# Attention and two feed-forward layers on one core: masks in fewer operations, the first biases on VectorE, input words on another queue, a range test moved

## The chip, the cores and the metric

The kernel runs on one core of one Trainium2 chip. The metric is the device time of one execution in microseconds; lower is better. The compute engines are TensorE (PE in the profile, with its weight loads as PEld), VectorE (DVE), ScalarE (ACT) and GpSimd (POOL). SyncE (SP) only issues transfers; a name with a q, as SPq, is an engine's sequencer.

## The reference

The inputs are `q`, `k`, `v` of 2 batches, 8 heads, 768 positions and 64 dimensions, two integers `n_global` (8) and `n_local` (96), and two pairs of float64 weight matrices. A query sees a key if the key is among the first `n_global` or at most `n_local - 1` positions back:

```python
scores = scale * np.matmul(q, k.transpose(0, 1, 3, 2))
rel = pos[:, None] - pos[None, :]
is_global = pos[None, :] < int(n_global)
is_local = (rel >= 0) & (rel < int(n_local))
keep = is_global | is_local
dist = np.where(is_global & ~is_local, float(n_local), np.abs(rel))
scores = np.where(keep, scores - slopes[:, None, None] * dist, -1000000000.0)
a = softmax(scores); attn_out = np.matmul(a, v)
```

The result, as 1536 tokens of 512 channels, goes through two layers: `h = x @ w_in`, a gate (`h * sigmoid(h)` in the first, `h * clip(h + 3, 0, 6) / 6` in the second), `@ w_out`.

## The kernel before

The two integers are read on the chip, so the masks are made there. The kernel serves small values of both; at the end a flag tells whether the integers lie beyond that range, and a general version (`every_key`) runs if they do. Here they don't.

**The start.** The first block of code sets three warm-up matmuls going on TensorE (`warm_up(3)`), issues the transfers of the integers' words (`nwords`) and of the first units' inputs on SP's queue (`loads`, `loads_v`), and makes the masks on VectorE. `positions()` writes relative positions by GpSimd and converts them on VectorE. `patterns()` waits for the words, makes `ng` and `nl` of them, and writes two tiles of penalised distances: `distB` for the 128 keys of a block's own, and `distA` for 256 columns, which hold the 96 keys before, 32 global keys and the block's own. A key that is not kept gets at least the distance `FAR`. `biases(p)` multiplies both tiles with the slopes of the two heads of pair `p`, four operations on GpSimd, which gives `nbB` and `nbA`.

**Attention.** A unit is a batch, half of its positions and a pair of heads: 16 units, each in three steps of one query block. For every unit the keys and queries are transposed by TensorE (`stage_a`, into `psA`) and copied by ScalarE to `kt` and `qt`, with a small copy of the global keys by VectorE (L332). TensorE computes the scores (L359), VectorE adds the bias and takes the extreme (L370, into `z` and `mn`), ScalarE exponentiates (L374), GpSimd divides by the sums (L384), TensorE transposes the weights (`turn`, into `psT`), VectorE and ScalarE copy them to `pt`, and TensorE multiplies them with the values (`values`, `psO`). Steps are counted by `n`; `attention_loop(n)` runs them three to a unit, and `biases(u + 1)` comes with the first step of units 0 to 2.

**Feed-forward.** From step 17 on, matmul pieces of the first layer (`psH`, `psY`) are mixed in, and the float64 weights are fetched raw on SP's queue and decoded to two float32 parts by ScalarE, VectorE and GpSimd (`decode`, L103 to L148 and L983 to L1000).

**Order.** During attention TensorE, ScalarE and GpSimd follow the written order; the first block and, until attention ends, VectorE are ordered by a planner with costs of its own, which also orders SP's queue throughout. So an operation that is written late can come early: the range test `beyond()` is written at step 30, but its six operations run between those of `patterns()`. After attention VectorE follows the written order too. At step 77 all five sequencers read the flag that `beyond()` writes (L786):

```python
if n == PRE + 60:
    general = nc.values_load(flag[0:1, 0:1], min_val=0, max_val=2)
```

The functions that the diff touches, and their callers, with the profile's line numbers:

Of the kernel before, what the change touches and what calls it, by code (L numbers as in the profile page):

```python
# [10 lines left out]
F32 = mybir.dt.float32  # L11
F32R = mybir.dt.float32r
I32 = mybir.dt.int32
U32 = mybir.dt.uint32
AF = mybir.ActivationFunctionType
ALU = mybir.AluOpType
PSUM = bass.MemoryType.PSUM

P = 128
# [9 lines left out]
def attention_ffn_kernel(ctx, tc, q, k, v, n_global, n_local, w_in1, w_out1, w_in2, w_out2, out):  # L29
    nc = tc.nc  # L30
# [15 lines left out]
    keep = ctx.enter_context(tc.tile_pool(name="keep", bufs=1))  # L46
    ident = keep.tile([P, P], F32, name="ident", tag="ident")
    nval = keep.tile([P, 2], F32, name="nval", tag="nval")
    flag = keep.tile([P, 1], I32, name="flag", tag="flag")
    three = keep.tile([P, 1], F32, name="three", tag="three")  # L50

    main = ExitStack()
    first_half, second_half = ExitStack(), ExitStack()
    cpool = first_half.enter_context(tc.tile_pool(name="const", bufs=1, side="right"))
# [143 lines left out]
    PRE = 3 * NP + LAG + 1  # L198
# [50 lines left out]
    slopes = [2.0 ** (-8.0 * (h + 1) / H) for h in range(H)]  # L249
    FAR = 1e9 / slopes[-1]  # L250

    small = cpool.tile([P, 5], F32, name="small", tag="small")
    t1 = apool.tile([P, HB, 2, W], F32, name="pat1", tag="z", bufs=ZB)[:, 0]
    t2 = apool.tile([P, HB, 2, W], F32, name="pat2", tag="z", bufs=ZB)[:, 0]
    rel, tmp, glob, col = distA, t2[:, 0, :], t2[:, 1, :P], t2[:, 1, P:]

    def positions():

        reli, coli = t1[:, 0, :].bitcast(I32), t1[:, 1, :P].bitcast(I32)
        nc.gpsimd.iota(reli[:, :P], pattern=[[-1, P]], base=G0, channel_multiplier=1)  # L260
        nc.gpsimd.iota(reli[:, P:], pattern=[[-1, P]], base=0, channel_multiplier=1)
        nc.gpsimd.iota(coli, pattern=[[1, P]], base=0, channel_multiplier=0)
        nc.vector.tensor_copy(rel, reli)
        nc.vector.tensor_copy(col, coli)
        nc.vector.tensor_scalar(out=tmp, in0=rel, scalar1=0.0, scalar2=None, op0=ALU.is_ge)

    def patterns():

        low, up, high = nwords[:, :, 0], nwords[:, :, 1], small[:, 0:2]
        nc.vector.scalar_tensor_tensor(out=high, in0=low, scalar=0.0, in1=up, op0=ALU.is_lt, op1=ALU.add)  # L270
        nc.vector.scalar_tensor_tensor(out=nval, in0=high, scalar=4294967296.0, in1=low, op0=ALU.mult, op1=ALU.add)
        ng, nl = nval[:, 0:1], nval[:, 1:2]
        nc.vector.tensor_scalar(out=glob, in0=col, scalar1=ng, scalar2=None, op0=ALU.is_lt)
        nc.vector.scalar_tensor_tensor(out=tmp, in0=rel, scalar=nl, in1=tmp, op0=ALU.is_lt, op1=ALU.mult)

        def mask(dist, kept):
            nc.vector.tensor_scalar(out=kept, in0=kept, scalar1=-FAR, scalar2=FAR, op0=ALU.mult, op1=ALU.add)
            nc.vector.tensor_tensor(out=dist, in0=dist, in1=kept, op=ALU.max)


        nc.vector.scalar_tensor_tensor(out=distB, in0=rel[:, P:], scalar=nl, in1=tmp[:, P:], op0=ALU.subtract, op1=ALU.mult)
        nc.vector.tensor_scalar(out=distB, in0=distB, scalar1=nl, scalar2=None, op0=ALU.add)
        nc.vector.tensor_tensor(out=col, in0=tmp[:, P:], in1=glob, op=ALU.max)
        mask(distB, col)

        nc.vector.tensor_copy(tmp[:, G0:P], glob[:, :G])
        nc.vector.tensor_scalar(out=rel[:, G0:P], in0=rel[:, G0:P], scalar1=0.0, scalar2=nl, op0=ALU.mult, op1=ALU.add)
        mask(rel, tmp)

    def beyond():  # L290

        fl, ng, nl = small[:, 2:5], nval[:, 0:1], nval[:, 1:2]
        nc.vector.tensor_scalar(out=fl[:, 0:1], in0=nl, scalar1=1.0, scalar2=None, op0=ALU.is_lt)
        nc.vector.tensor_scalar(out=fl[:, 1:2], in0=nl, scalar1=float(NLOC_MAX), scalar2=None, op0=ALU.is_gt)
        nc.vector.tensor_scalar(out=fl[:, 2:3], in0=ng, scalar1=float(NGLOB_MAX), scalar2=None, op0=ALU.is_gt)
        nc.vector.tensor_tensor(out=fl[:, 0:1], in0=fl[:, 0:1], in1=fl[:, 1:2], op=ALU.add)
        nc.vector.tensor_tensor(out=fl[:, 0:1], in0=fl[:, 0:1], in1=fl[:, 2:3], op=ALU.add)
        nc.vector.tensor_copy(flag, fl[:, 0:1])
# [3 lines left out]
    def biases(p):  # L302

        nbs[p] = [cpool.tile([P, 2, w], F32, name=f"{n}{p}", tag=f"{n}{p}") for n, w in (("nbB", P), ("nbA", W))]
        for nb, dist in zip(nbs[p], (distB, distA)):
            for h in range(2):
                nc.gpsimd.tensor_scalar(out=nb[:, h, :], in0=dist, scalar1=slopes[2 * p + h], scalar2=1.0, op0=ALU.mult, op1=ALU.mult)


    KW = HB * SP  # L310
# [2 lines left out]
    def stage_a(u, part):  # L313

        b, half, p = units[u]
        rk, rq, rv, vp = raw[u]
        if part == 0:
            tr[u] = tuple(apool.tile([P, w], F32, name=f"{n}{u}", tag=n) for n, w in (("kt", KW), ("qt", TB)))
        kt, qt = tr[u]
        ps = bank("tr", f"psA{u}_{part}")  # L320
        src = rq if part else rk
        for i in range(HB):
            nc.tensor.transpose(ps[:, i * P:(i + 1) * P], src[:, i].rearrange("p h d -> p (h d)"), ident)
        if part:
            nc.scalar.mul(qt, ps[:, :TB], -1.0 / (D ** 0.5))
            return
        kt3 = kt.rearrange("p (t c) -> p t c", t=HB)
        nc.scalar.copy(kt3[:, :, :P], ps[:, :TB].rearrange("p (t c) -> p t c", t=HB))
        if half:
            nc.vector.tensor_copy(kt3[:, :HB - 1, P:], kept[b, p][:, G0:].unsqueeze(1).to_broadcast([P, HB - 1, G]))  # L330
        else:
            nc.vector.tensor_copy(kt3[:, :, P:], ps[:, :G].unsqueeze(1).to_broadcast([P, HB, G]))  # L332
            kept[b, p] = cpool.tile([P, P], F32, name=f"kept{u}", tag=f"kept{p}")
            nc.gpsimd.tensor_scalar(out=kept[b, p], in0=kt[:, KW - P:], scalar1=1.0, scalar2=1.0, op0=ALU.mult, op1=ALU.mult)
# [94 lines left out]
    def attention_loop(n):  # L429
        u, t = divmod(n, HB)  # L430
        for f in queue.pop(n, []):
            f()
        if u < len(units):
            if t == 0:
                scores(u)
                if u + 1 < NP:
                    biases(u + 1)
            exponentials(u, t)
            if t:
                normalise(u, *((0, 2), (2, 3))[t - 1])  # L440
        if t == 0 and 0 <= u - 2 < len(units):
            at(n + 1, values(u - 2))
            if u < len(units):
                loads_v(u)
        if n == 30:
            beyond()
        for f in rests.pop(n, []):
            f()
        if n == 2:
            warm_up(2)  # L450
        if t < 2 and u + 1 < len(units):
            stage_a(u + 1, t)
            if t and u + 3 < len(units):
                loads(u + 3)
# [277 lines left out]
    with tc.manual_schedule(engines=None):  # L732
        nc.vector.memset(three, 3.0)
        warm = fpool.tile([P, 512], F32, name="warm", tag="a")
        nc.vector.memset(warm, 0.0)
        warm_up(3)
        for i, ap in enumerate((n_global, n_local)):
            nc.sync.dma_start(nwords[:, i, :], ap.bitcast(I32).partition_broadcast(P))
        loads(0)
        make_identity(nc, ident)  # L740
        positions()
        loads(1)
        load_weights()
        loads_v(0)
        load_weights()
        loads(2)
        loads_v(1)
        load_weights()
        patterns()
        biases(0)  # L750
        stage_a(0, 0)
        stage_a(0, 1)
    todo = {when(i): f for i, f in enumerate(stream)}

    def loop(n):
        now[0] = n
        attention_loop(n)
        f = todo.get(n)
        if f:
            f[0](*f[1:])  # L760
        turns(n)
        for f in late.pop(n, []) + slots.pop(n, []):
            f()
# [8 lines left out]
    with tc.manual_schedule(engines={E.PE, E.Activation, E.Pool, E.DVE}):  # L772

        first_half.close()
        late_pool = second_half.enter_context(tc.tile_pool(name="late", bufs=1, side="right", reuse_waits="tile"))
        for b in range(2):
            whole_block(b)
        for n in range(end, when(len(stream) - 1) + 2):
            if n == when(first_piece[0, 3]):
                ready[0] = 2  # L780
            for l, c, early in ((0, 2, 0), (1, 1, 6)):
                if n == when(first_piece[l, c]) - early:
                    block_sums(l, n, n + early + 12)
            loop(n)
            if n == PRE + 60:
                general = nc.values_load(flag[0:1, 0:1], min_val=0, max_val=2)  # L786
    second_half.close()
# [245 lines left out]
```

## Time and profile before

| | us |
|---|---|
| median of 3 runs | 622.43 (622.29 to 622.67) |
| the profiled execution | 621.98 |
| its span, first to last instruction | 619.9 |
| TensorE busy | 599.9 (97% of the span) |
| VectorE, ScalarE, GpSimd busy | 471.5, 414.6, 161.4 |

A time line row gives the start, the duration, the engine, the line, the operation, what is written and read, how many instructions are merged, and in brackets the engine's idle time before it with what ended it. The durations of neighbours on one engine can overlap. A wait for several semaphores is put down to the one that came last by the profile.

### The profile page before, as it was taken

How to read it: one execution, taken by the hardware profiler on the slowest of the kernel's cores; microseconds unless marked ns; L12 is line 12 of the kernel's file. 1: busy time of each engine (PE TensorE's matmuls, PEld its weight loads, DVE VectorE, ACT ScalarE, POOL GpSimd, SP SyncE). 2: the span in 40 equal slices, each digit the busy share in tenths (PEclk: the TensorE clock that was granted, in tenths of full speed). 3: DMA queues.
4: the chain of work that ended last, by engine and by line, in shares of the span. 5: the costliest groups of instructions: out<-in, count | busy, mean ns of one | idle time of the engine just before them, and what ended most of it. 6: DMA issues, size and time to landing. Idle time of an engine off the chain costs nothing.

```text
span 619.9 us, 9396 instructions
## 1 busy us (share of the span) xinstructions
PE 599.9 (97%) x3144; PEld 492.1 (79%) x3144; DVE 471.5 (76%) x1036; ACT 414.6 (67%) x863; POOL 161.4 (26%) x241
## 2 busy tenths in 40 slices
PE   7789999999999999999999999999999999999996
PEld 3577788898887888888888878887788888888884
DVE  6988888636697767677766789987979797969453
ACT  4888888655576757575757776666667675757660
POOL 3987676821111111111111200011021112121200
PEclk9999999999999999999999999999999999999999
DMA  7876654584776777777777872476587777776544
GB/s 182 189 163 143 147 139 107 191 152 107 155 169 136 170 169 170 168 172 163 177 160 146 173 167 68 159 177 174 135 176 165 173 166 171 169 170 136 103 119 158
DMA packets 78679, 96.64 MB, mean 156 GB/s; under 512 B 52512, under 2 KB 52512, under 8 KB 78368
## 3 DMA queue, kind: packets, MB, share of 16 engines
q0 software_dynamic: 12576, 45.09, 38.9%
q1 hardware_dynamic: 66048, 50.87, 28.1%
q8 instruction: 27, 0.44, 0.3%
q14 instruction: 28, 0.23, 0.1%
HBM read 45.62 MB, written 3.15 MB: 79 GB/s over the span
## 4 chain that ended last, share of the span: by engine, by line
PE 36%; issue 26%; POOL 5%; DVE 2%; DMA 2%; ACT 1%; POOLq 0%; ACTq 0%; SPq 0%; DVEq 0%
PE psY L653 20%; PE psH L480 9%; POOL y L682 5%; PE psP_b L561 3%; PE psP_c L561 2%; PE psP_a L561 2%; DMA y<-st 1%; DMA raw<-in_moe_w_in_dram 1%; ACT st L678 0%; DVE g L511 0%; DVE da L995 0%; DVE wol L148 0%; DVE u L578 0%; DVE dc L134 0%; ACT da L103 0%
## 5 line engine op out<-in xcount | busy, mean ns | idle before, releaser
L682 POOL DMA_DIRECT2D y<-st x78 | 66.9, 858 | 364.9 <-ACT st L678 359.7
L678 ACT COPY st<-psY 128x512 f32<-128x512 f32 x156 | 91.5, 587 | 51.9 <-PE psY L653 47.9
L480 PE MATMUL psH<-xh,wih 128*128 128x512 f32 (+1 forms) x216 | 83.0, 384 | 1.2 <-DVE g L511 0.7
L480 PE MATMUL psH<-xh,wil 128*128 128x512 f32 (+1 forms) x216 | 82.5, 382 | 0.4 <-POOL wil L148 0.4
L480 PE MATMUL psH<-xl,wih 128*128 128x512 f32 (+1 forms) x216 | 82.6, 382 | 0.2 <-DVE xl L416 0.2
L653 PE MATMUL psY<-gh,woh 128*128 128x512 f32 (+1 forms) x160 | 61.4, 384 | 0.6 <-DVE mn L370 0.6
L653 PE MATMUL psY<-gh,wol 128*128 128x512 f32 (+1 forms) x160 | 60.6, 379 | 0.0
L653 PE MATMUL psY<-gl,woh 128*128 128x512 f32 (+1 forms) x160 | 60.5, 378 | 0.0
L653 PE MATMUL psY<-woh,gh 128*128 128x512 f32 x144 | 56.1, 390 | 0.5 <-ACT gh L517 0.5
L653 PE MATMUL psY<-woh,gl 128*128 128x512 f32 x144 | 56.1, 390 | 0.2 <-DVE gl L524 0.2
L653 PE MATMUL psY<-wol,gh 128*128 128x512 f32 x144 | 56.0, 389 | 0.0
L374 ACT ACTIVATE z<-z,mn 128x256 f32<-128x256 f32 (+1 forms) x96 | 46.3, 487 | 9.8 <-DVE mn L370 9.3
L384 POOL TENSOR_SCALAR z<-z,sm 128x256 f32<-128x256 f32 (+1 forms) x96 | 43.7, 475 | 21.4 <-DVE sm L380 16.0
L480 PEld LDWEIGHTS psH<-xh,wih 128*128 128x128 f32 x216 | 40.5, 188 | 9.5 <-ACT y L667 1.2
L103 ACT ACTIVATE da<-raw 128x512 f32<-128x512 f32 x64 | 43.0, 672 | 6.4 <-DMA raw<-in_moe_w_in_dram 5.9
L480 PEld LDWEIGHTS psH<-xl,wih 128*128 128x128 f32 x216 | 40.6, 188 | 7.9 <-DVE xl L416 0.5
L480 PEld LDWEIGHTS psH<-xh,wil 128*128 128x128 f32 x216 | 40.5, 188 | 8.0 <-POOL wil L148 0.8
L995 DVE SCALAR_TENSOR_TENSOR da<-raw,da 128x512 int32<-128x512 int32 x64 | 45.9, 717 | 1.0
L983 DVE TENSOR_SCALAR da<-da 128x512 f32<-128x512 f32 x64 | 29.8, 466 | 16.3 <-ACT da L103 16.2
L578 DVE TENSOR_TENSOR u<-psP_c,u 128x512 f32<-128x512 f32 x22 | 15.1, 688 | 34.5 <-ACT u L572 34.5
L502 ACT ACTIVATE a<-psH 128x512 f32<-128x512 f32 (+1 forms) x24 | 14.2, 590 | 40.3 <-PE psH L480 40.3
L521 DVE SCALAR_TENSOR_TENSOR gl<-a,gh 128x512 fp32r<-128x512 f32 (+1 forms) x34 | 23.2, 682 | 22.3 <-ACT gh L515 22.0
(186 smaller groups left out, 1497.8 us busy)
## 6 DMA issues: line engine op xcount, KB each, us to landing
y<-st POOLq DMA_DIRECT2D x78, 512.0 KB, 4.9
raw<-in_moe_w_in_dram SPq DMA_DIRECT2D x32, 512.0 KB, 4.2
raw<-in_moe_w_out_dram SPq DMA_DIRECT2D x32, 512.0 KB, 3.5
rk<-in_k_dram SPq DMA_DIRECT2D x32, 96.0 KB, 3.3
rq<-in_q_dram SPq DMA_DIRECT2D x32, 96.0 KB, 3.1
rv<-in_v_dram SPq DMA_DIRECT2D x32, 96.0 KB, 2.4
out_dram<-y SPq DMA_DIRECT2D x12, 256.0 KB, 2.3
xf<-xh SPq DMA_DIRECT2D x2, 1024.0 KB, 5.3
```

The costliest lines, as they stand in the source:

```text
L103: nc.scalar.activation(out=t["a"], in_=raws[n][:, :, 1].bitcast(F32), func=AF.Abs)
L374: nc.scalar.activation(out=z[:, t, h, :w], in_=z[:, t, h, :w], func=AF.Exp, bias=mn[:, t, h:h + 1], scale=-1.0, accum_out=sm[:, t, h:h + 1])
L384: nc.gpsimd.tensor_scalar(out=z[:, t, h, :w], in0=z[:, t, h, :w], scalar1=smt[u][:, t, h:h + 1], scalar2=1.0, op0=ALU.mult, op1=ALU.mult)
L480: nc.tensor.matmul(ps, a[:, kt, js], x[:, kt, n0:n1], start=n == 0, stop=n == 3 * KT - 1)
L521: nc.vector.scalar_tensor_tensor(out=gl[:, j, :], in0=t["a"], scalar=2.0, in1=gh[:, j, :].bitcast(F32), op0=ALU.mult, op1=ALU.subtract)
L561: nc.tensor.matmul(ps, a[:, 2 * k + q, f * P:(f + 1) * P], x, start=p in (1, 5) and n == 0, stop=n == 5, skip_group_check=True)
L578: nc.vector.tensor_tensor(out=u, in0=st["c"], in1=u, op=ALU.add)
L653: nc.tensor.matmul(ps[:, :rhs.shape[1]], lhs, rhs, start=n == 0, stop=n == 3 * FC - 1)
L678: nc.scalar.copy(st[:, m % 2, :], part)
L682: late.setdefault(n, []).append(lambda: nc.gpsimd.dma_start(y, st, accum_op=ALU.add))
L983: nc.vector.tensor_scalar(out=a, in0=a, scalar1=as_float(897 << 20), scalar2=as_float((1151 << 20) - 1), op0=ALU.max, op1=ALU.min)
L995: nc.vector.scalar_tensor_tensor(out=ai, in0=w1, scalar=-0x40000000, in1=ai, op0=ALU.bitwise_and, op1=ALU.bitwise_or)
```

## The change

Masks: the tests are negated (1 where a key is not kept), so that a fused operation can multiply them with `FAR` and add the distance at once; the helper `mask` goes, and three operations on the 128-column tile and two on the 256-column tile change. The maximum with `FAR` becomes a sum. Biases: those of pair 0 are made by VectorE, the others by GpSimd as before. Words: their two transfers are issued by ScalarE. The first `stage_a(0, 0)` is written ahead of `biases(0)`. The range test gets a tile of its own and is written at step 73 of the stage behind the attention, where VectorE follows the written order.

```diff
-    rel, tmp, glob, col = distA, t2[:, 0, :], t2[:, 1, :P], t2[:, 1, P:]
+    rel, tmp, glob, col, near = distA, t2[:, 0, :], t2[:, 1, :P], t2[:, 1, P:], t1[:, 1, P:]
-        nc.vector.tensor_scalar(out=tmp, in0=rel, scalar1=0.0, scalar2=None, op0=ALU.is_ge)
+        nc.vector.tensor_scalar(out=tmp, in0=rel, scalar1=0.0, scalar2=None, op0=ALU.is_lt)
...
-        nc.vector.tensor_scalar(out=glob, in0=col, scalar1=ng, scalar2=None, op0=ALU.is_lt)
-        nc.vector.scalar_tensor_tensor(out=tmp, in0=rel, scalar=nl, in1=tmp, op0=ALU.is_lt, op1=ALU.mult)
-
-        def mask(dist, kept):
-            nc.vector.tensor_scalar(out=kept, in0=kept, scalar1=-FAR, scalar2=FAR, op0=ALU.mult, op1=ALU.add)
-            nc.vector.tensor_tensor(out=dist, in0=dist, in1=kept, op=ALU.max)
-
-        nc.vector.scalar_tensor_tensor(out=distB, in0=rel[:, P:], scalar=nl, in1=tmp[:, P:], op0=ALU.subtract, op1=ALU.mult)
-        nc.vector.tensor_scalar(out=distB, in0=distB, scalar1=nl, scalar2=None, op0=ALU.add)
-        nc.vector.tensor_tensor(out=col, in0=tmp[:, P:], in1=glob, op=ALU.max)
-        mask(distB, col)
-
-        nc.vector.tensor_copy(tmp[:, G0:P], glob[:, :G])
-        nc.vector.tensor_scalar(out=rel[:, G0:P], in0=rel[:, G0:P], scalar1=0.0, scalar2=nl, op0=ALU.mult, op1=ALU.add)
-        mask(rel, tmp)
+        own, V = slice(P, W), nc.vector
+        V.scalar_tensor_tensor(out=tmp, in0=rel, scalar=nl, in1=tmp, op0=ALU.is_ge, op1=ALU.max)
+        V.tensor_scalar(out=glob, in0=col, scalar1=ng, scalar2=None, op0=ALU.is_ge)
+        V.scalar_tensor_tensor(out=near, in0=rel[:, own], scalar=nl, in1=tmp[:, own], op0=ALU.subtract, op1=ALU.mult)
+        V.tensor_tensor(out=near, in0=rel[:, own], in1=near, op=ALU.subtract)
+        V.tensor_tensor(out=col, in0=glob, in1=tmp[:, own], op=ALU.mult)
+        V.scalar_tensor_tensor(out=distB, in0=col, scalar=FAR, in1=near, op0=ALU.mult, op1=ALU.add)
+
+        V.tensor_copy(tmp[:, G0:P], glob[:, :G])
+        V.tensor_scalar(out=rel[:, G0:P], in0=rel[:, G0:P], scalar1=0.0, scalar2=nl, op0=ALU.mult, op1=ALU.add)
+        V.scalar_tensor_tensor(out=distA, in0=tmp, scalar=FAR, in1=rel, op0=ALU.mult, op1=ALU.add)
 
     def beyond():
 
-        fl, ng, nl = small[:, 2:5], nval[:, 0:1], nval[:, 1:2]
+        fl, ng, nl = beyonds, nval[:, 0:1], nval[:, 1:2]
...
-                nc.gpsimd.tensor_scalar(out=nb[:, h, :], in0=dist, scalar1=slopes[2 * p + h], scalar2=1.0, op0=ALU.mult, op1=ALU.mult)
+                (nc.gpsimd if p else nc.vector).tensor_scalar(out=nb[:, h, :], in0=dist, scalar1=slopes[2 * p + h], scalar2=1.0,
+                                                              op0=ALU.mult, op1=ALU.mult)
...
-        if n == 30:
-            beyond()
...
-            nc.sync.dma_start(nwords[:, i, :], ap.bitcast(I32).partition_broadcast(P))
+            nc.scalar.dma_start(nwords[:, i, :], ap.bitcast(I32).partition_broadcast(P))
...
         patterns()
+        stage_a(0, 0)
         biases(0)
-        stage_a(0, 0)
         stage_a(0, 1)
...
+            if n == PRE + 56:
+                beyond()
             if n == PRE + 60:
                 general = nc.values_load(flag[0:1, 0:1], min_val=0, max_val=2)
```

## Rows read from the trace of the kernel before

**Rows 1.** Stretches: length, then busy us of PE, PEld, DVE, ACT, POOL.
```profile
14.14:30.20 16.06, 12.45 (x115) 8.95 (x112) 14.73 (x62) 14.21 (x49) 15.60 (x31) 1.00 0.81 188
...
120.00:350.00 230.00, 229.43 (x1044) 191.54 (x1045) 157.46 (x282) 145.76 (x267) 38.55 (x43) 1.00 0.72 159
```

**Rows 2.** Time line of TensorE, 0 to 16 us.
```profile
1.51 5.59 PE L421 MATMUL psW<-warm 128*128 128x512 f32 x6 [1.51 <-DVE warm L735]
6.94 0.49 PE L323 MATMUL psA<-ident,rk 128*128 128x128 f32 x3
...
8.39 0.93 PE L359 MATMUL psS_S<-kt,qt 64*128 64x128 f32 x8 [0.63 <-ACT qt L325]
...
13.18 0.93 PE L359 MATMUL psS_S<-kt,qt 64*128 64x128 f32 x8 [0.58 <-ACT qt L325]
...
15.50 0.52 PE L323 MATMUL psA<-ident,rq 128*128 128x128 f32 x3 [0.42 <-DMA rq<-in_q_dram]
```

**Rows 3.** Time line of ScalarE, 0 to 16 us.
```profile
0.76 1.28 ACT L328 ACT_TABLE_LOAD   x1 [0.76 <-PEq L1015]
...
7.84 0.50 ACT L325 ACTIVATE qt<-psA 128x384 f32<-128x384 f32 x1
```

**Rows 4.** Time line of VectorE, 0 to 16 us.
```profile
4.78 0.16 DVE L270 SCALAR_TENSOR_TENSOR small<-nwords 128x2 f32<-128x2 int32 x1 [2.41 <-DMA nwords<-in_n_local_dram]
...
5.38 0.48 DVE L274 SCALAR_TENSOR_TENSOR pat<-distA,nval,pat 128x256 f32<-128x256 f32 x1
5.78 0.15 DVE L293 TENSOR_SCALAR small<-nval 128x1 f32<-128x1 f32 x1
...
5.90 0.35 DVE L281 SCALAR_TENSOR_TENSOR distB<-distA,nval,pat 128x128 f32<-128x128 f32 x1
...
6.49 0.29 DVE L283 TENSOR_TENSOR pat<-pat 128x128 f32<-128x128 f32 x1
...
6.81 0.23 DVE L277 TENSOR_SCALAR pat<-pat 128x128 f32<-128x128 f32 x1
...
7.51 0.40 DVE L277 TENSOR_SCALAR pat<-pat 128x256 f32<-128x256 f32 x1
...
8.29 0.25 DVE L332 COPY kt<-psA 128x96 f32<-128x96 f32 x1
9.46 0.29 DVE L370 CUSTOM_DVE_ANT_0 z<-psS_S,nbB 128x128 f32<-128x128 f32 x1 [0.92 <-POOL nbA L307]
...
14.14 0.29 DVE L370 CUSTOM_DVE_ANT_0 z<-psS_S,nbB 128x128 f32<-128x128 f32 x1 [0.17 <-PE psS_S L359]
```

**Rows 5.** Line 307 (biases), 0 to 30 us: count, ns min/median/max, first and last start.
```profile
L307 POOL TENSOR_SCALAR nbB<-distB x8: 294/299/499, 7.5 to 23.0; 128x128 f32<-128x128 f32 x8
L307 POOL TENSOR_SCALAR nbA<-distA x8: 406/408/907, 9.0 to 23.8; 128x256 f32<-128x256 f32 x8
```

**Rows 6.** Time line of SP's queue, 0 to 16 us.
```profile
0.76 0.39 SPq L738 DMA_DIRECT2D nwords<-in_n_global_dram  x1
...
1.67 0.96 SPq L228 DMA_DIRECT2D rk<-in_k_dram  x2
```

**Rows 7.** What TensorE waited for, 0 to 120 us: us in total, times, longest.
```profile
PE psT L394 <- DVE pt L399: 1.8, 3, 1.0
...
PE psO L412 <- DVE pt L399: 1.0, 1, 1.0
PE psA L323 <- DMA rq<-in_q_dram: 0.8, 2, 0.4
```

**Rows 8.** Line 786, the reads of the flag: count, ns, first and last start.
```profile
L786 SPq TENSOR_LOAD <-flag x1: 480/480/480, 45.6 to 45.6; - x1
...
L786 PEldq TENSOR_LOAD <-flag x1: 807/807/807, 161.0 to 161.0; - x1
```

**Rows 9.** Time line of VectorE, 155 to 163 us.
```profile
160.94 0.69 DVE L148 TENSOR_TENSOR wol<-dc,woh 128x512 fp32r<-128x512 f32 x1 [2.31 <-ACT woh L145]
```

**Rows 10.** Line 983 (a decode step), 0 to 40 us: count, ns min/median/max.
```profile
L983 DVE TENSOR_SCALAR da<-da x3: 427/868/967, 11.8 to 35.7; 128x512 f32<-128x512 f32 x3
```

More of the change, by code (lines that the diff above doesn't have):

```diff
@@ L49, in attention_ffn_kernel @@
     flag = keep.tile([P, 1], I32, name="flag", tag="flag")
+    beyonds = keep.tile([P, 3], F32, name="beyonds", tag="beyonds")
     three = keep.tile([P, 1], F32, name="three", tag="three")
@@ L250, in attention_ffn_kernel @@
     FAR = 1e9 / slopes[-1]
-    small = cpool.tile([P, 5], F32, name="small", tag="small")
+    small = cpool.tile([P, 2], F32, name="small", tag="small")
     t1 = apool.tile([P, HB, 2, W], F32, name="pat1", tag="z", bufs=ZB)[:, 0]
     t2 = apool.tile([P, HB, 2, W], F32, name="pat2", tag="z", bufs=ZB)[:, 0]
-    rel, tmp, glob, col = distA, t2[:, 0, :], t2[:, 1, :P], t2[:, 1, P:]
+    rel, tmp, glob, col, near = distA, t2[:, 0, :], t2[:, 1, :P], t2[:, 1, P:], t1[:, 1, P:]
     def positions():
```

## The prediction

> **What bounds the kernel now.** I read the stretches of the span first [rows 1]. From 120 to 350 us TensorE is busy 229.43 of 230.00 us: there only a change of TensorE's own work can pay. From 14.14 to 30.20 us it is busy 12.45 of 16.06, and GpSimd 15.60. All edits but one lie before 10 us. So the question is whether time saved there reaches TensorE, and whether it survives the stretch in which GpSimd is full.
>
> Then the time lines of the start. TensorE begins with the warm-up matmuls, from 1.51 us for 5.59, that is until 7.10; the first transposes follow at 6.94 without a wait shown [rows 2]. ScalarE's second copy of their results runs from 7.84 for 0.50 us [rows 3], and behind it, at 8.39, the first scores start [rows 2]. Their first eight matmuls take 0.93 us, until 9.32. VectorE's first addition of the bias starts at 9.46 [rows 4]. The trace puts its wait of 0.92 us down to GpSimd's bias tile, but it can only start behind the scores too. For the next unit the same step starts at 14.14, waiting for scores that began at 13.18 [rows 2, 4]: 13.18 plus 0.93 is 14.11, so it is 0.03 us behind them, against 0.14 here. GpSimd's biases hold up the first unit by at most 0.14 less 0.03, **0.11 us**.
>
> VectorE's mask work stands beside this chain, not in it: it waits 2.41 us for the input words, starts at 4.78 and is done when the key copy, at 8.29, has taken its 0.25: 8.54 [rows 4].
>
> **The change, part by part.**
>
> *Masks.* Before, VectorE ran 20 instructions from 4.78 to 8.54. Their durations sum to 4.93 us in 3.76 us, so neighbours overlap and a duration costs 0.76 of itself (a row of each kind stands in [rows 4], the first and the last of the 20 among them; six, of 0.15 to 0.16, are the range test). Afterwards, at those durations: two word operations 0.32, two fused operations on 256 columns 0.96, two on 128 columns 0.70, two with two tensors on 128 columns 0.58, one test on 128 columns 0.23, two short ones at no more than that 0.46, the key copy 0.25. Together 3.50 us.
>
> *First biases by VectorE.* The trace has no such step on this engine. The nearest are its operations with two constants, 0.23 us on 128 columns and 0.40 on 256 [rows 4]; two of each are 1.26. With the masks 4.76, times 0.76, 3.62: VectorE is done at 8.40. If nothing overlapped it would be 4.78 plus 4.76, 9.54. The scores end at 9.32 all the same, so I take nothing lost, and half of the 0.11 gained: **-0.05**. The upper bound: the key copy, which half of the eight score matmuls need, is planned last and ends at 9.54; half of 0.93 and the 0.03 follow, and the first bias step starts at 10.04 instead of 9.46, **+0.6**.
>
> *GpSimd relieved.* Four instructions go, two of about 0.30 and two of 0.41 us [rows 5], 1.4 us. They lie before 9.75, and GpSimd's full stretch begins only at 14.14, with the first unit's normalisation; that moves as the first unit does, so they count 0.
>
> *Input words on ScalarE's queue.* SP issues the words from 0.76 us and the first key load at 1.67 [rows 6], so all its early loads may come 0.9 us sooner. For unit 0 that is worth nothing: its transposes wait for the warm-up. Up to 120 us TensorE waits 0.8 us in all for query loads [rows 7], 0.42 of it at 15.50 [rows 2]. I count **-0.15** of that: GpSimd's and ScalarE's work of unit 0 and 1 is still under way behind it, so most of it would turn into another wait. The ends are 0 and -0.8. ScalarE is idle until its copies apart from a table load of 1.28 us [rows 3]; if the words were issued behind it, they would land 1.28 later, VectorE would be done at 9.68 instead of 8.40, and the first step would be 0.2 late, or 0.7 with the key copy last.
>
> The Trainium skill, DMA: Bandwidth & Descriptors, "Issuing engines are not separate DMA queues", says that issuing from several engines saves only issue time, since all transfers end on the same 16 DMA engines. By it, too, those 0.9 us are all that is to be had, and the words now meet the first key loads there; no row shows how much later they then land.
>
> *Range test.* Six instructions leave the gaps of the masks and go to step 73 of the loop, near 158 us, where VectorE sits idle for 2.31 us before 160.94 [rows 9]. Six of 0.16, not overlapped, are 1.0 us: hidden, and without that gap 1.0 us of VectorE where TensorE hardly waits for it. The flag is read by TensorE's sequencer at 161.0 us and by SP at 45.6 [rows 8]. SP must now wait for it until about 160; the weight loads behind it wait, by the code, for VectorE to have read an older piece, which it does after the test as well. I take 0; a test that came late by more than TensorE's queue holds would add what it is late.
>
> **Sum.** -0.05 and -0.15 are **-0.2 us** on the profiled execution's 621.98 us (a span of 619.9, with 2.1 around it). The median shown, 622.43, is 0.45 above that execution, so the forecast is 622.2. Measurements of this kernel tell about 0.2%, 1.24 us, from no change: I forecast no change, 621.7 to 622.6 with the small terms at their ends.
>
> **Rivals.** *(a) The shared port.* VectorE's new biases run beside GpSimd's biases of unit 1. One and the same VectorE operation takes 427 ns in one place and 967 in another [rows 10], and GpSimd's bias step 406 to 907 [rows 5], while both are busy. If each of four biases grew by 0.54, VectorE would be done at 8.40 plus 2.16, 10.56, and the first step would start 1.1 us late: 623.3. If they only waited for GpSimd's four steps, 1.4 us, it would be 9.80, 0.35 late, 622.6. Against it: GpSimd may be through with its own first. The Trainium skill, SBUF — State Buffer, "SBUF: two separate sides", has VectorE and GpSimd hold a shared pair of ports exclusively for a whole instruction, the loser waiting; by that rule the lower of the two prices holds, since the loser waits once for each step of the other.
>
> *(b) VectorE's order turns out better, and the time faster.* Up to about 120 us a planner orders VectorE and SP by its own clock, and a new head moves that clock. TensorE waits there 1.8 and 1.0 us for VectorE's copies of transposed weights [rows 7]; a decode step of 0.97 us planned ahead of such a copy makes such a wait [rows 10]. If half of the 2.8 went, with the loads' gain: -1.6, 620.8.
>
> *(c) The same order turns out worse, and the time slower.* One more decode step ahead of a copy costs up to 1.0 us [rows 7]; from two on it decides: +2.0 less 0.2, 624.2. VectorE is busy 14.73 of 16.06 us there [rows 1], so its order matters, for (b) and (c); against both, no work changes after 9.46 us.
>
> **Chances.** Forecast 0.58; (a) 0.12, within 0.2% as well; (b) 0.20; (c) 0.10. So faster 0.20, same 0.70, slower 0.10. The range is 620.8, the middle of (b), to 623.3, the top of (a), with the bound of +0.6 inside: it leaves out half of (b) and all of (c), 0.2.
>
> **What would show it.** After the change the warm-up should still end near 7.1 us and the first scores start near 8.4, the first bias step 0.9 to 1.1 us behind that, with VectorE done before; the first key load issued near 0.8; GpSimd's full stretch begin near 14.0; the range test sit in VectorE's gap before 161 us with no wait of TensorE. The prediction is wrong if TensorE's waits for VectorE from 14 to 120 us change by more than a microsecond, if the key copy comes behind the biases, or if masks start later than about 5.7 us, where the cover of 0.95 us (9.35 less 8.40) is used up.

## The result, and the profile after

| | before | after |
|---|---|---|
| median of 6 runs, lowest to highest (us) | 622.50, 621.90 to 623.88 | 626.57, 625.92 to 626.97 |
| ratio, 95% interval | | 1.0054, 1.0042 to 1.0065 |
| span of the profiled execution (us) | 619.9 | 623.8 |
| TensorE busy (us) | 599.9 | 605.4 |

The change makes the kernel 0.5% slower, about 4 us, where no change was forecast; 626.57 lies above the range and above the time of every rival. Below, ratios are compared and not times: the kernel before was timed again beside each group of experiments, and its medians lie from 622.5 to 623.4 us.

The stretches after, as in [rows 1]: TensorE is as full as before from 120 to 350 us, at the same granted clock, and GpSimd nearly as full from 14 to 30.

```profile
14.14:30.20 16.06, 12.71 (x116) 9.05 (x114) 13.89 (x64) 14.25 (x50) 15.19 (x31) 1.00 0.77 182
120.00:350.00 230.00, 229.68 (x1039) 190.32 (x1038) 156.49 (x286) 144.12 (x265) 38.43 (x43) 1.00 0.70 158
```

One number differs: in the same 230 us TensorE does 1039 matmuls instead of 1044. It is busy, and slower.

TensorE's time line of the start, beside [rows 2], and VectorE's, beside [rows 4]:

```profile
1.50 6.17 PE L419 MATMUL psW<-warm 128*128 128x512 f32 x6 [1.50 <-DVE warm L731]
...
8.96 0.93 PE L357 MATMUL psS_S<-kt,qt 64*128 64x128 f32 x8 [0.63 <-ACT qt L323]
...
15.31 0.49 PE L321 MATMUL psA<-ident,rq 128*128 128x128 f32 x3
...
17.04 1.06 PE L392 MATMUL psT<-ident,z 128*128 128x128 f32 x8 [1.02 <-DVE kt L330]
```
```profile
4.93 0.16 DVE L271 SCALAR_TENSOR_TENSOR small<-nwords 128x2 f32<-128x2 int32 x1 [2.56 <-DMA nwords<-in_n_local_dram]
...
8.55 0.26 DVE L330 COPY kt<-psA 128x96 f32<-128x96 f32 x1 [0.73 <-ACT kt L326]
8.72 0.43 DVE L304 TENSOR_SCALAR nbB<-distB 128x128 f32<-128x128 f32 x2
9.07 0.59 DVE L304 TENSOR_SCALAR nbA<-distA 128x256 f32<-128x256 f32 x2
9.92 0.29 DVE L368 CUSTOM_DVE_ANT_0 z<-psS_S,nbB 128x128 f32<-128x128 f32 x1 [0.26 <-PE psS_S L357]
```

The warm-up ends at 7.67 instead of 7.10, and all behind it is 0.57 later. The first bias step is 0.96 behind the first scores (1.07 before).

SP's queue, what TensorE waits for up to 120 us, and the range test (VectorE's time line, then the reads of the flag), beside [rows 6 to 9]:

```profile
0.76 0.98 SPq L229 DMA_DIRECT2D rk<-in_k_dram  x2
```
```profile
PE psT L392 <- DVE pt L397: 1.5, 3, 0.6
...
PE psT L392 <- DVE kt L330: 1.0, 1, 1.0
```
```profile
158.43 0.15 DVE L295 CAST flag<-beyonds 128x1 int32<-128x1 f32 x1
158.50 0.68 DVE L993 SCALAR_TENSOR_TENSOR da<-raw,da 128x512 int32<-128x512 int32 x1
160.93 0.69 DVE L149 TENSOR_TENSOR wol<-dc,woh 128x512 fp32r<-128x512 f32 x1 [1.74 <-ACT woh L146]
```
```profile
L784 SPq TENSOR_LOAD <-flag x1: 476/476/476, 158.6 to 158.6; - x1
...
L784 PEldq TENSOR_LOAD <-flag x1: 760/760/760, 161.0 to 161.0; - x1
```

None of this costs 4 us: TensorE's waits from 14 to 120 us sum to 7.3 us (8.5 before), those of them for VectorE to 4.8 (5.5). To find the place I took the start of the n-th matmul after, less that of the n-th before, all along the span: +0.55 us at 17 us, +0.06 at 46, about +0.1 up to 115, -0.01 from 155 to 196. Up to there the change has caught up with its late start. From 224 us on the difference grows, to about +1.6 at 347 us, stands still from 370 to 420, and reaches +4.11 at the end. Where it grows, TensorE works through the Strassen products: a layer's first matmul in seven block products in place of eight, some of them of sums and differences of blocks. `psP_a`, `psP_b` and `psP_c` collect them; `t2`, `t3`, `t4` are sums of the tokens (`xh`, `xl`), `ws` of the weights (`wih`, `wil`). Between them lies the layer's second matmul (`psY`, of the gated `g` and the weights `woh`, `wol`). The chain that ended last shows them in sixes; columns are start, length, what. First before, then after, the same work:

```profile
448.22 2.72 PE psY L653 x12
450.94 1.36 PE psP_b L561 x6
452.30 1.36 PE psY L653 x6
453.66 1.36 PE psP_c L561 x6
...
459.10 1.36 PE psP_a L561 x6
```
```profile
449.98 2.80 PE psY L649 x12
452.78 1.39 PE psP_b L557 x6
454.16 1.40 PE psY L649 x6
455.56 1.40 PE psP_c L557 x6
...
461.14 1.36 PE psP_a L557 x6
```

Six matmuls take 1.36 us in every piece before, 227 ns from the start of one to the start of the next; this is called their spacing below. After, they take 1.39 to 1.40 in some pieces, a spacing of 232 to 233, and 1.36 in others. One matmul overlaps the next, so its own duration is longer than the spacing. The durations of one product (count, ns min/median/max, first and last start), before and after:

```profile
L561 PE MATMUL psP_c<-xh,ws x80: 389/389/389, 228.5 to 590.6; 128*128 128x512 f32 x80
```
```profile
L557 PE MATMUL psP_c<-xh,ws x80: 389/396/400, 228.6 to 594.5; 128*128 128x512 f32 x80
```

The same matmul, on the same tiles, waits for nobody and is 7 ns longer. Slow are the 462 products that read one tile of the pool opened late, on the right of the memory (`ws`, `g`, `t4`), and one from the left (`xh`, `xl`, `wih`, `wil`, `woh`, `wol`), and some right behind them. What the change does to these is in one line of the diff: the tile `beyonds`, 12 bytes, allocated ahead of the left tiles, for which the compiled program keeps 32 bytes. The bytes of a partition at which the compiled program has tiles start (of `wih` and `woh`, one of two buffers):

```
          xh      wih     woh     |  g       ws      t4h
before    17120   117472  133856  |  172000  180192  217056    all 224 modulo 256
after     17152   117504  133888  |  172000  180192  217056    left 0, right 224 modulo 256
```

### The profile page after: what moved, and what is told of

Its sections match the earlier page's. It is cut to its first block, busy times and chain, and to the rows that moved or that the text cites. A ratio compares the mean times of both kernels' runs of the same rounds, so it can differ in the third digit from the quotient of the medians.

```text
span 623.8 us, 9395 instructions
## 1 busy us (share of the span) xinstructions
PE 605.4 (97%) x3144; PEld 492.5 (79%) x3144; DVE 471.1 (76%) x1038; ACT 415.1 (67%) x863; POOL 159.7 (26%) x237
## 4 chain that ended last, share of the span: by engine, by line
PE 36%; issue 26%; POOL 5%; DVE 2%; DMA 2%; ACT 1%; POOLq 0%; ACTq 0%; SPq 0%; DVEq 0%
PE psY L649 20%; PE psH L476 9%; POOL y L678 5%; PE psP_b L557 3%; PE psP_c L557 2%; PE psP_a L557 2%; DMA y<-st 1%; DMA raw<-in_moe_w_in_dram 1%; ACT st L674 0%; DVE g L507 0%; DVE da L993 0%; DVE wol L149 0%; DVE u L574 0%; DVE dc L135 0%; ACT da L104 0%
```

## The experiments

**Theory:** a product is faster when its moving operand and its weights start at the same byte modulo some power of two. **Rivals:** the new order of the start and the later test shift the loads against TensorE's reads; or the later warm-up. In a name as `psP_c<-xh,ws` the moving operand stands first, the weights behind it.

*The shift alone*, in the kernel before: a tile that nobody uses.

```
     three = keep.tile([P, 1], F32, name="three", tag="three")
+    keep.tile([P, 8], F32, name="pad", tag="pad")
```

> The kernel before, with nothing else than that tile of 32 bytes beside the flag's: the left tiles start at a multiple of 64 bytes, the late ones from the right 32 past one. Theory A: 626.5 us (ratio to before 1.006 to 1.007), with spacings of about 233 ns in the products and pieces that read a late tile, and 227 elsewhere, from 224 us on. Theories B and C: 622.5 us (ratio 1.000), since head, order and range test are those of before.

Measured: 627.6 us, ratio 1.0075 (1.0057 to 1.0093). The matmuls are 0.75 us late at 17 us and 0.74 at 196, then ever later, up to +5.03; the same 462 products take 3.1 us more than before, as in the change. 32 idle bytes do it, with order, start and test as before.

*Two other distances:* the same line in the changed kernel (left tiles 64 bytes further than before), and the changed kernel with an idle tile of 32 bytes ahead of the late pool instead, which moves the right tiles.

```
+        second_half.enter_context(tc.tile_pool(name="shift", bufs=1, side="right")).tile([P, 8], F32, name="pad", tag="pad")
```

> The changed kernel with 32 bytes more per partition in front of the tiles that are allocated from the left (a further tile of eight columns beside the flag's), so that these tiles again start 32 bytes past a multiple of 64, as before the change, and as the late tiles from the right do. Theory A (the new tile of the range test moved the left tiles by 32 bytes, and matmuls with one operand on either side of that offset run 3% slower): matmul spacing 227 ns throughout, time 622.5 us (ratio to before 0.999 to 1.001). Theory B (the loss comes from another order or timing of the other engines after the changed head): nothing of that is altered, so 626.5 us (ratio 1.0065). Theory C (the biases and words at the start cost it): 626.5 as well.

> The changed kernel with 32 bytes taken from the right end ahead of the late tiles, so that left and late tiles both start at multiples of 64 bytes. Theory A, in the form that only the difference of the two counts: 622.5 us (ratio 0.999 to 1.001). Theory A2 (a start that is a multiple of 64 is itself the slow one): slower than the changed kernel, 630 us or more, since all matmuls then have it. Theories B and C: 626.5 us.

Measured: 625.77, ratio 1.0042 (1.0028 to 1.0057), and 626.19, ratio 1.0050 (1.0033 to 1.0067). My first form of the theory, that 64 bytes would do, fell, and so did the rival that a start at a multiple of 64 is itself slow (630 us). But the spacing now depends on which of the two operands is the left one. Where the weights start 192 bytes ahead of the moving operand (modulo 256) it is 229.8 ns (`psP_c`) and 229.1 (moving `woh`, weights `g`); where they start 64 ahead it is 233.3 (moving `t4`, weights `wih`) and 233.4 (moving `g`, weights `woh`).

*A later head:* a longer warm-up in the kernel before.

```
-        warm_up(3)
+        warm_up(4)
```

> The kernel before with four warm-up matmuls in place of three, so that TensorE's first transposes, and all that follows from them, start later by one such matmul, 0.9 to 2.1 us. If time at the head is taken up by slack before 50 us, as the traces before and after suggest (0.55 us late at 17 us, 0.06 at 46 us, nothing at 161 us), the time stays at 622.5 us (ratio 0.999 to 1.001). If the head's chain carried through to the end, 623.4 to 624.6 us (ratio 1.0015 to 1.0035).

Measured: 624.02, ratio 1.0022 (1.0007 to 1.0036). In the profile the matmuls are 1.55 us late at 17 us, 1.51 at 370 and 1.38 at the end; every product stays at 227. A late head is carried through to the end, but once: the rival of the later warm-up can't make a difference that grows.

*Only matmuls,* no attention and no experts; moving operand and weights start 64 bytes apart modulo 256, or 32 or 96 when one of them is moved by 8 columns.

```
run("evenEven", [(0, 0)] * 48)
run("evenOdd", [(0, 1)] * 48)
...
run("mixed", ([(0, 0)] * 6 + [(0, 1)] * 6) * 6)
```

> Leaves out the whole computation (it writes zeros) and runs only matmuls of 512 columns in fp32r, 128 by 128 weights loaded for each, with no other engine at work. Tiles start at a multiple of 64 bytes (even) or 32 past one (odd); named by moving operand, then weights, 48 matmuls each: evenEven, evenOdd, oddEven, oddOdd; then sixes of evenEven and oddOdd in turn, and sixes of evenEven and evenOdd in turn. Theory A (the offset between moving operand and weights is enough): 227 ns in evenEven and oddOdd, about 233 in evenOdd and oddEven. Theory A3 (it takes another engine's accesses beside): 227 ns everywhere. Whether a matmul after a slow one stays slow shows in the sixes.

```profile
L42 PE MATMUL evenOdd<-moving,weight 128*128 128x512 f32 x48 | 11.4, 396 | 0.0
L42 PE MATMUL evenEven<-moving,weight 128*128 128x512 f32 x48 | 11.4, 396 | 0.0
```

All sections run at about 233 ns, since no pair here has equal starts. It shows that the slow spacing needs no other engine at work and no transfer, and it separates nothing else.

*The change without the shift:* the flags lie in the unused bytes behind `nval`.

```
-    nval = keep.tile([P, 2], F32, name="nval", tag="nval")
-    beyonds = keep.tile([P, 3], F32, name="beyonds", tag="beyonds")
+    tests = keep.tile([P, 5], F32, name="nval", tag="nval")
+    nval, beyonds = tests[:, 0:2], tests[:, 2:5]
```

> The changed kernel, whole, but the three flags of the range test lie in the unused bytes behind nval instead of in a tile of their own, so that xh, the weights and everything behind them start at the bytes at which the kernel before has them. Theory (start addresses: a product runs at 227 ns if the moving operand and the weights start at the same byte modulo 128 or 256, and at 230 to 235 otherwise): the products with late tiles are 227 ns apart again, nothing is lost after 224 us, and the 0.6 us that the edits gain between 17 and 46 us stay: 621.9, between 621.3 and 622.5, a ratio of 0.998 to 1.000. Rival (the new order of the head or the range test's place sets the slow spacing): 626.5, ratio 1.006, products at 233 ns as in the changed kernel.

Measured: 622.36, ratio **0.9985 (0.9976 to 0.9993)**, median of before in that comparison 623.33. All else of the change is in it, and the products are back:

```profile
L557 PE MATMUL psP_c<-xh,ws 128*128 128x512 f32 x80 | 27.9, 389 | 0.0
```

The rival order is out: the order is here, the loss is not. *The period:* before with 128 idle bytes, and the change with 224 more (256 in all).

```
+    keep.tile([P, 32], F32, name="pad", tag="pad")
...
+    keep.tile([P, 56], F32, name="pad", tag="pad")
```

> The kernel before with an idle tile of 128 bytes at the place of the new one, so that the left tiles and the late ones start 128 bytes apart modulo 256 and equal modulo 128. Theory with a period of 128 bytes: products at 227 ns, 622.5 us, ratio 1.000. Theory with a period of 256 bytes: products with late tiles at about 233 ns, 626 to 627.6 us, ratio 1.006. Rival (any move of the tiles costs, whatever the distance): 627.6 as with 32 bytes.

> The changed kernel, whole, with an idle tile of 224 bytes behind the new one of 32, so that the left tiles start 256 bytes further than in the kernel before. Theory (equal start modulo 256 bytes): the products with late tiles at 227 ns, no loss after 224 us, a ratio of 0.9985 like that of the changed kernel without the shift, between 0.997 and 1.000. Rival (a tile more in the pool, or any bytes but those of before, cost): ratio 1.005, products at 233 ns.

Measured: 626.85, ratio 1.0053 (1.0038 to 1.0067), the 462 products at 232 to 233 ns on the mean; and 621.72, ratio **0.9977 (0.9966 to 0.9988)**, products at 227. A move of 256 bytes costs nothing, one of 128 does: the period is 256 bytes. From here on, a product whose two operands start at the same byte modulo 256 is called equal, any other unequal. Both versions of the change without unequal products are faster than both kernels; their intervals overlap, so they are not told apart.

*The table.* 24 matmuls a section, the weights' start moved in steps of 32 bytes (A to P), then the moving operand's, then both.

```
for w in range(16): run("weight" + chr(65 + w), 0, w)
for w in range(8):  run("moving" + chr(65 + w), w, 0)
for w in range(8):  run("both" + chr(65 + w), w, w)
```

> Only matmuls, 24 in a section, all 512 columns wide: the weights' start moved against the moving operand's by 0 to 480 bytes in steps of 32 (weightA to weightP), then the moving operand's against the weights' by 0 to 224 (movingA to movingH), then both together (bothA to bothH); no attention, no experts. Theory: 227 ns where the two are equal modulo 128 (A, E, I, M, and all of both), or modulo 256 alone (A, I), and 230 to 236 at the others, with a difference of 64 less dear than 32 or 96. Rival (absolute address, or the kernel's other engines): no such table; one number for all, or both changes with its letter.

Groups of TensorE by section (busy us, mean ns of one); A is 0 bytes apart, B 32, E 128, G 192, I 256:

```profile
L38 PE MATMUL weightE<-moving,weight 128*128 128x512 f32 x24 | 5.8, 395 | 0.0
...
L38 PE MATMUL weightB<-moving,weight 128*128 128x512 f32 x24 | 5.8, 395 | 0.0
L38 PE MATMUL weightG<-moving,weight 128*128 128x512 f32 x24 | 5.7, 392 | 0.0
...
L38 PE MATMUL movingC<-moving,weight 128*128 128x512 f32 x24 | 5.7, 392 | 0.0
...
L38 PE MATMUL bothE<-moving,weight 128*128 128x512 f32 x24 | 5.6, 390 | 0.0
...
L38 PE MATMUL weightA<-moving,weight 128*128 128x512 f32 x24 | 5.6, 389 | 0.0
L38 PE MATMUL weightI<-moving,weight 128*128 128x512 f32 x24 | 5.6, 389 | 0.0
```

From start to start: 226.7 ns at 0 and 256 bytes, 227.8 with both moved, 233.1 to 234.1 at every other distance but one: 229.3 where the weights are 192 ahead (G, O, and movingC, where the moving operand is 64 ahead). That one distance is what the two runs with 64 bytes had for `psP_c` and `woh` on `g`. Beyond 256 bytes the values repeat (B and J, C and K, and so on). The rival of an absolute address is out. The 227.8 is a mean: in the sections bothB to bothH the first seven products are 224 to 236 ns apart, the others 226 to 227. Each of these sections stands behind one of equal products too, whose two starts lie 32 bytes lower. So a change of start from one product to the next can make equal products slow for a while, without any unequal one. Where the section before has the same starts (weightA, behind the first matmuls of the run), all products are 226 to 227 apart.

*Behind unequal products.* 1, 2, 6 and 12 unequal products (128 bytes) between 24 equal ones; then two starts in turn, equal within a product and unequal to the neighbour (straight), or the reverse (crossed).

```
for letter, n in zip("ABCD", (1, 2, 6, 12)):
    run("equal" + letter, [(0, 0)] * 24)
    run("unequal" + letter, [(0, 1)] * n)
...
run("straight", [(0, 0), (1, 1)] * 24)
run("crossed", [(0, 1), (1, 0)] * 24)
```

> Only matmuls of 512 columns: 24 products whose moving operand and weights start equal modulo 256 bytes, then 1, 2, 6 and 12 whose weights start 128 bytes further, each followed by 24 equal ones; then two starts in turn, first equal within each product and unequal to the neighbour's (straight), then unequal within each product and equal to the neighbour's weights (crossed); no attention, no experts. If the slow spacing belongs to the unequal products alone: 233 ns for those, 227 for every equal one behind them, straight 227, crossed 233. If the products behind them run on slowly for a while, as the trace of the changed kernel suggests (about six between 459.6 and 461.0 us): 20 to 25 ns more in all in the first six of each equal section behind unequal ones. If what counts is one product's moving operand against the weights loaded for the next: straight 233, crossed 227.

Spacings in ns, worked out from the starts:

```
behind 1 unequal    227 227 226 227 ...
behind 2            235 233 236 224 231 236 228 233 231 | 226 227 ...
behind 6            231 227 226 227 ...
behind 12           236 224 231 236 228 232 231 | 227 227 ...
straight, mean of 48: 228.6      crossed, mean of 48: 230.2
```

Equal products can run on slowly, up to nine of them, 47 ns in all (2087 less nine times 226.7), but not always. Neither reading of the pair holds alone: straight and crossed both lie between 227 and 233. In straight every product is equal and every start differs from the one before.

*Where the gain comes from:* the kernel before with the first biases by VectorE, behind the first key copy, and nothing else.

```
-                nc.gpsimd.tensor_scalar(out=nb[:, h, :], in0=dist, scalar1=slopes[2 * p + h], scalar2=1.0, op0=ALU.mult, op1=ALU.mult)
+                (nc.gpsimd if p else nc.vector).tensor_scalar(out=nb[:, h, :], in0=dist, scalar1=slopes[2 * p + h], scalar2=1.0, op0=ALU.mult, op1=ALU.mult)
-        biases(0)
         stage_a(0, 0)
+        biases(0)
```

> The kernel before with two edits of the change alone: the first biases by VectorE, and issued behind the first key copy. If these bring the 0.6 us that the changed kernel gains between 17 and 46 us: 621.9, ratio 0.999, the shift of the matmuls against before falling by 0.6 us between 17 and 46 us. If the masks' fewer operations or the words' queue bring it: 622.5 to 623, ratio 1.000 to 1.001, and no such fall.

Measured: 622.79, ratio 0.9989 (0.9979 to 0.9998); the matmuls come from +0.40 us at 17 us to -0.16 at 46. The same fall, 0.47 to 0.56 us, stands in all six profiles with these two edits, and not in the three of kernels without them (0.02 to 0.09). So they bring most of what the change gains; masks, words and test together bring at most a small rest, which these intervals do not tell from nothing. Time lines of GpSimd and VectorE around the place where most of it arises, before and with this edit:

```profile
32.74 0.94 POOL L384 TENSOR_SCALAR z<-z,sm 128x256 f32<-128x256 f32 x2 [0.55 <-DVE mn L370]
33.64 1.28 POOL L126 TENSOR_TENSOR dc<-dc,de 128x512 f32<-128x512 f32 x1
```
```profile
33.83 1.13 DVE L330 COPY kt<-kept 128x64 f32<-128x64 f32 x1
34.88 0.55 DVE L416 TENSOR_TENSOR xl<-psO,xh 128x384 fp32r<-128x384 f32 x1
```
```profile
32.62 0.93 POOL L384 TENSOR_SCALAR z<-z,sm 128x256 f32<-128x256 f32 x2 [0.22 <-DVE sm L380]
33.52 1.28 POOL L126 TENSOR_TENSOR dc<-dc,de 128x512 f32<-128x512 f32 x1
```
```profile
34.08 0.77 DVE L330 COPY kt<-kept 128x64 f32<-128x64 f32 x1
34.77 0.55 DVE L416 TENSOR_TENSOR xl<-psO,xh 128x384 fp32r<-128x384 f32 x1
```

VectorE's copy of 64 columns ends 0.04 us behind GpSimd's operation in one trace (33.83 + 1.13 against 33.64 + 1.28) and 0.05 in the other. All eight copies of this kind in the trace of before (count, ns min/median/max, first and last start):

```profile
L330 DVE COPY kt<-kept x8: 181/241/1132, 20.4 to 98.2; 128x64 f32<-128x64 f32 x8
```

The four that run while GpSimd does nothing take 0.18 to 0.19 us, the four beside a GpSimd operation 0.29 to 1.13, and each of these four ends 0.04 to 0.05 us behind one. So this copy stands until GpSimd is done with that operation. GpSimd's wait ahead of its two rows is 0.33 us shorter (0.22 for 0.55), so VectorE's `xl` comes sooner, and TensorE's wait for it falls from 0.79 us to 0.42. The traces of the change with and without the shift show the same copy at 0.77 us. The Trainium skill, SBUF — State Buffer, "SBUF: two separate sides", states such a port, held for a whole instruction; both traces agree. Why GpSimd is released sooner is open: behind the first biases TensorE, VectorE, ScalarE and GpSimd have the same instructions in the same order.

## Why the prediction was wrong

**The step that failed is the range test's**, "I take 0". Its instructions were priced, and rightly: the flag is there at 158.6 us, when SP reads it, and TensorE reads it at 161.0 as before and is no later than before up to 196 us. Its tile was not priced. The sum has no term for what a new tile moves, and [rows 1] had said where such a term would count: from 120 us on TensorE is never idle, and only a change of its own work tells there. The tile made 462 products unequal (132 in `psP_c`, 66 with `t4`, 264 with `g`). From start to start these take 3.1 us more in the trace, 6.7 ns each; the other 1.0 of the 4.1 lies in equal products among and around them. Of that 0.6 is in `psP_b` with `t2` and `t3`, whose two operands are both late tiles and which still take 392 to 394 ns instead of 389. That the tile is the cause is shown by the change without the shift (ratio 0.9985, against 1.0054 with it), by the shift alone (1.0075) and by the shift of 256 bytes (0.9977). Why unequal products are slower is open.

None of the prediction's signs of being wrong came. TensorE's waits for VectorE from 14 to 120 us changed by 0.7 us, the key copy came ahead of the biases, and VectorE began on the words at 4.93. All three watch waits or the head of the span, and the loss is in neither.

**Masks and first biases.** Hidden, as forecast, but not for the reason given: VectorE is done at 9.66, not 8.40, since the key copy waits 0.73 us for ScalarE and the biases come behind it. The first bias step still waits for the scores, and gains the 0.11 us that were its bound; I took 0.05. All six profiles with the edit have it 0.96 us behind the first scores, the four without 1.07 to 1.08. The edit is worth some 0.5 us more between 17 and 46 us, where I had priced GpSimd's relief at 0 because the work lay before its full stretch. This term was mis-sized: -0.05 against about -0.7 (0.9989 of 623.3; by the interval, -0.1 to -1.3).

**Input words.** The first key load is issued at 0.76, as forecast. TensorE's wait for the query at 15.50 is gone, and the next transposes wait 1.02 us for a key copy instead of 0.25: they start 0.55 late at 17.04, where the scores before them, at 13.64, were 0.46 late. From 14 to 120 us the waits for query loads fall from 0.8 us to 0.2, and those for key loads rise from 0.2 to 0.7. "Most of it would turn into another wait" held; of the -0.15 nothing is to be seen. The words' transfers were issued ahead of ScalarE's table load, and VectorE starts on them 0.15 later.

**The warm-up** was to end near 7.1 and ended at 7.67. Its code is the same, and in the profiles of all kernels with this warm-up it ended between 6.75 and 7.84 (the latter in the kernel before with only the idle tile); so this scatters from one program or execution to another. The longer warm-up shows that such an offset goes through to the end. It also means that spans of single profiles, 619.9 of before among them, compare poorly: the last matmul of the change without the shift comes 0.1 us later than there, and its median is 0.97 lower.

**Rivals.** (a) did not come at its place: VectorE's four bias steps took 0.94 us from start to end, GpSimd was through with its own 0.2 us after they began, and the first bias step was not late. The port shows 25 us later, at a copy that waits for GpSimd before and after, and there the change gains. For (b), 620.8, the mechanism was another order of VectorE; the order is the same, and of what the versions without a shift gain, the largest piece seen in the traces is a port that comes free sooner. (c) did not happen. No rival had TensorE's own work change, so 0.1 for slower was too little.

## What to carry to other kernels

A new tile is an edit of every tile behind it. Where TensorE is the bound, compare the duration of the same matmul by tile in both traces before looking for a wait: a median of 389 against 396 ns tells it in one row. Put small tiles where there is padding, as here behind `nval`, or fill up to 256 bytes; what counts is that moving operands and weights start at the same byte modulo 256, and from one product to the next too. This holds for what ran here: fp32r matmuls of 512 columns with new weights for each.

## What the runs showed of the hardware

- 512-column fp32r matmuls with a new weight load each follow one another after 226.7 ns if both operands start at the same byte modulo 256, after 229.3 if the weights are 192 ahead, and after 233.1 to 234.1 at every other multiple of 32 that was tried, at a granted clock of 1.00 and with no other engine busy.
- The Trainium skill, SBUF — State Buffer, "Who interferes with whom", gives TensorE separate ports for moving operand and weights and names one shared port pair, VectorE's and GpSimd's, as the only contention. Here TensorE alone at work runs up to 3% slower (234.1 against 226.7 ns) by where its two operands start, and the measurement decides; which part of the chip causes it, no run shows.
- Behind unequal products up to nine equal ones ran slowly (224 to 236 ns), in some patterns and not in others. Behind equal ones that start 32 bytes lower, the first seven did. What decides is open.
- A copy of 64 columns on VectorE took 0.18 to 0.19 us with GpSimd idle, and up to 1.13 beside a GpSimd operation, until that was done.
